# Six of eight chunks of the last up piece, with the upper partitions' half rows moved to the lower ones and loaded from GpSimd's queue

## The chip, the cores and the metric

One NeuronCore of one Trainium2 chip runs the whole program. The metric is the device time of one execution in microseconds; the kernel before has a median of 2686.6 us over three runs. A profiled execution gives the trace from which the lines below come; its own span is 2685.0 us.

## The reference

Two layers, run twice in turn on two tokens (B = 2, one position each, D = 576): attention over a cache of 8192 positions with 32 heads of 128, and a gated mlp with 4608 inner columns. Everything is float32.

```python
def _A_ref(x, k_cache, v_cache, wq, wo):
    q = (x @ wq).reshape(B, Sq, H, Dh).transpose(0, 2, 1, 3)
    scores = einsum("bhqd,bhkd->bhqk", q, k_cache) * (Dh ** -0.5)
    o = einsum("bhqk,bhkd->bhqd", softmax(scores), v_cache)
    return o.transpose(0, 2, 1, 3).reshape(B, Sq, H * Dh) @ wo
def _B_ref(x, w_gate, w_up, w_down):
    g, u = x @ w_gate, x @ w_up
    return (gelu(g) * u) @ w_down
x = x + _A_ref(layernorm(x), k_cache, v_cache, wq, wo)
x = x + _B_ref(layernorm(x), w_gate, w_up, w_down)
x = x + _A_ref(layernorm(x), k_cache, v_cache, wq, wo)
x = x + _B_ref(layernorm(x), w_gate, w_up, w_down)
```

The caches (2 x 268 MB, read in both layers but for some parts that are kept) and the weights make 1153 MB that go from HBM to the core.

## The kernel before

**One large tile.** Keys, values and weights all lie in one SBUF tile, `space`, of 128 partitions by 50,176 columns. The class `Arena` hands out column ranges of it when the program is built. Each load is a function `make` in the list `queue`: `pump` (L148) runs them in order as long as the arena has room, and `done` (L152) frees a range when the last instruction that reads it has been written down, and pumps again. So the order of loads is the order of the list (`plan_first`, `plan_mlp(0)`, `plan_second`, `plan_mlp(1)`), all are issued from SP's queue, and each stands in the program as soon as its place is free. The waits between engines and transfers are put in by the framework, from which columns and partitions of a tile each instruction reads and writes. SP's loads use eight completion semaphores, in turn.

**The second attention's end.** VectorE multiplies keys with the query, GpSimd adds halves (L661), VectorE sums the rest, ScalarE takes the exponential, TensorE multiplies with the values (L762). `project` (L807) then multiplies with the eight pieces of `wo`, and `add_to_x` (L520) adds the result to `x`.

**The second mlp** (`mlp`, L931, with `split` false). `norm` (L486) centres `x`, transposes it into `xt` (128 partitions by 6 + 288 columns; each of nine blocks of 32 columns holds one set of half rows) and lets GpSimd compute `rstd` (L517), which ScalarE first needs in `activate` (L976). The gate and up matrices, 576 by 4608, are read as 1152 half rows of 2304: partition p holds half rows 9p to 9p + 8. `half_rows` (L221) loads them; gate in three transfers of three half rows a partition (3456 KB each), up in two such and three single ones (1152 KB each), as `GU` says. In `all_products` (L959) each half row on the partitions is cut into eight chunks of HG = 288 columns, and one product per chunk, with eight columns of `xt` as weights, adds into the PSUM tile `acc`; `window` picks the columns so that the even and the odd half rows fall on different rows of `acc`. A product in float32 shows as two matmul instructions in the trace. The last piece, the single one with u = 8, is the "ninth half row" of the change: its half rows on even partitions are first halves of a row of up, those on odd partitions second halves.

After it `activate` (L973) runs once for each half of the columns, and the down products (L1004) follow in eight parts, as their weights land (`down`, L264, issued at L271), with idle products (L526) between the first of them. `add_to_x` and two stores end the program.

Of the kernel before, what the change touches and what calls it, by code (L numbers as in the profile page):

```python
# [9 lines left out]
F32 = mybir.dt.float32  # L10
# [31 lines left out]
RING = 5 * SLOT  # L42
END = RING + NPLACE * PLACE
HELD = 5


class Item:
# [75 lines left out]
def decode_layers(ctx, tc, x_in, kc, vc, wq, wo, wg, wu, wd, out):  # L123
# [19 lines left out]


    arena = Arena()
    queue, ready, places = [], {}, {}

    def pump():  # L148
        while queue and queue[0]():
# [2 lines left out]
    def done(key):  # L152
        arena.free(key)
        pump()
# [54 lines left out]
    def weights(key, n, first, transfers):  # L209

        def make():
            at = arena.ring(key, n) if first is None else arena.fit(key, n, first)
            if at is None:
                return False
            t = ready[key] = part_at(at, n)
            transfers(t)
            return True

        queue.append(make)

    def half_rows(key, w, us, first):  # L221

        width = w.shape[1] // 2
        rows = w.rearrange("r (s w) -> (r s) w", w=width).rearrange("(p u) w -> p u w", p=P)

        def transfers(t):
            nc.sync.dma_start(t.rearrange("p (u w) -> p u w", w=width), rows[:, us[0]:us[-1] + 1, :])

        weights(key, len(us) * width, first, transfers)

    def of_half(h, k):

# [166 lines left out]
    def plan_mlp(layer):  # L399
        if layer == 0:  # L400
            for h in range(2):
                for u in range(4):
                    split_rows("g", wg, h, u)
                split_middle(h)
                for u in range(4):
                    split_rows("u", wu, h, u)
        else:
            for g, (name, w) in enumerate((("g", wg), ("u", wu))):
                for us in GU[g]:
                    half_rows((name, layer, us[0]), w, us, 0)  # L410
        for rows in DOWN[layer]:
            down(layer, rows)

# [45 lines left out]

    xt = consts.tile([P, PAD + NU * 32], F32, name="xt")
    nc.vector.memset(xt, 0.0)


# [20 lines left out]
    def norm(split=False, then=None):  # L486
        stats = work.tile([P, 6], F32, name="stats")
        nc.vector.bn_stats(stats, x)
        apart = work.tile([P, 4, 6], F32, name="apart")
        nc.vector.tensor_mul(  # L490
            apart, stats.unsqueeze(1).to_broadcast([P, 4, 6]), strip.unsqueeze(2).to_broadcast([P, 4, 6])
        )
        every4 = small(P, 4 * 6)
        nc.tensor.matmul(every4, same, apart.rearrange("p c t -> p (c t)"), start=True, stop=True)
        mv = work.tile([P, 2], F32, name="mv")
        nc.vector.bn_aggr(mv, every4)
        xc = once.tile([P, CW, 2], F32, name="xc", tag="xc")
        xr = x.rearrange("p (m r) -> p r m", r=NU)
        xs = xc.rearrange("p w s -> p (w s)")
        if split:  # L500
            xm = xs[:, :5 * 32].rearrange("p (u m e) -> p u m e", u=5, e=2)
            parts = [(xm[:, 0:4, :, e], xr[:, 5 * e:5 * e + 4, :], 0) for e in range(2)]
            parts += [(xm[:, 4, :, e], xr[:, 4, :], e) for e in range(2)]
            xs = xs[:, :5 * 32].rearrange("p (u q) -> p u q", u=5)
        else:
            parts = [(xc[:, :, s], x, s) for s in range(2)]
            xs = xs.rearrange("p (q u) -> p u q", u=NU)
        for to, of_x, s in parts:
            nc.vector.tensor_scalar(to, of_x, mv[:, 0:1], side[:, s:s + 1], op0=ALU.subtract, op1=ALU.mult)
        u = xs.shape[1]  # L510
        nc.vector.transpose(xt[:, PAD:PAD + 32 * u].rearrange("p (u q) -> p u q", u=u), xs)
        if then is not None:
            then()
        ve = work.tile([P, 1], F32, name="ve")
        nc.vector.tensor_scalar_add(ve, mv[:, 1:2], EPS)  # L515
        rstd = work.tile([P, 1], F32, name="rstd")
        nc.gpsimd.tensor_tensor(out=rstd, in0=ve, in1=mhalf, op=ALU.pow)  # L517
        return rstd
# [409 lines left out]
        add_to_x()  # L928


    def mlp(layer):  # L931
        split = layer == 0
        rstd = norm(split)
        if split:
            idle_products(3)
        hT = once.tile([P, 2, NI, 2, 2, B], F32, name="hT", tag="xc")

        def window(u, at):

            return xt[:, PAD + 32 * u - at:PAD + 32 * u - at + 4 * B]  # L940

        def split_products(h):

            steps = [(("g", layer, h, u), u, 2, (0,)) for u in range(4)] + [(("gu", layer, h), 4, 1, (0, 1))]
            steps += [(("u", layer, h, u), u, 2, (1,)) for u in range(4)]
            for key, u, sides, gs in steps:
                w = ready.pop(key).rearrange("p (k c w) -> p k c w", c=4, w=HG)
                for k in range(2):
                    g, e = (k, 0) if u == 4 else (gs[0], k)
                    for c in range(4):  # L950
                        nc.tensor.matmul(
                            acc[32 * c:32 * c + 4 * B, h, :HG], window(u, 4 * g + 2 * e), w[:, k, c, :],
                            start=(key == steps[0][0] and k == 0), stop=(key == steps[-1][0] and k == 1),
                        )
                done(key)
                if key != steps[-1][0]:
                    idle_products(1)

        def all_products():  # L959

            for g, name in enumerate("gu"):
                for us in GU[g]:
                    w = ready.pop((name, layer, us[0])).rearrange("p (u v c w) -> p u v c w", v=2, c=4, w=HG)
                    for u in us:
                        for v in range(2):
                            for c in range(4):
                                nc.tensor.matmul(
                                    acc[32 * c:32 * c + 4 * B, v, :HG], window(u, 4 * g), w[:, u - us[0], v, c, :],
                                    start=(g == 0 and u == 0), stop=(g == 1 and u == NU - 1),
                                )  # L970
                    done((name, layer, us[0]))

        def activate(v):  # L973

            o = once.tile([P, 2, HG], F32, name="o", tag="row")
            nc.scalar.activation(o[:, 0, :], acc[:, v, :HG], AF.Copy, scale=rstd)  # L976
            gu = o[:, 1, :].rearrange("p (i r) -> p i r", i=NI)
            nc.vector.transpose(gu, o[:, 0, :].rearrange("p (m i) -> p i m", i=NI))  # L978
            g = gu[:, :, 0:4]
            a = once.tile([P, NI, 4], F32, name="ga", tag="part")  # L980
            nc.vector.tensor_mul(a, g, g)
            nc.vector.tensor_scalar(a, a, 0.044715, 1.0, op0=ALU.mult, op1=ALU.add)
            nc.vector.tensor_mul(a, a, g)
            nc.scalar.activation(a, a, AF.Tanh, scale=math.sqrt(2.0 / math.pi))
            nc.vector.scalar_tensor_tensor(a, a, 1.0, g, op0=ALU.add, op1=ALU.mult)
            nc.vector.tensor_mul(a, a, gu[:, :, 4:8])
            a, to = a.rearrange("p i (e b) -> p (i e) b", b=B), hT[:, v].rearrange("p i e s b -> p (i e) s b")
            nc.vector.tensor_scalar_mul(to[:, :, 0, :], a, 0.5)
            nc.scalar.mul(to[:, :, 1, :], a, 0.5)

        if not split:
            all_products()
        for v in range(2):
            if split:
                split_products(v)
            activate(v)
        for n, rows in enumerate(DOWN[layer]):
            if n < len(IDLE[layer]):
                idle_products(IDLE[layer][n])
            w = ready.pop(("d", layer, rows[0])).rearrange("p (i c) -> p i c", c=D)  # L1000
            for k, (t, i) in enumerate(rows):
                v, e = divmod(t, 2) if split else (t % 2, t // 2)
                for c in range(4):
                    nc.tensor.matmul(  # L1004
                        xps[32 * c:32 * c + 2 * B, :], hT[:, v, i, e, :, :].rearrange("p s b -> p (s b)"),
                        w[:, k, c * CW:(c + 1) * CW],
                        start=(rows is DOWN[layer][0] and k == 0), stop=(t, i) == (NT - 1, NI - 1),
                    )
            done(("d", layer, rows[0]))
        add_to_x()  # L1010
        if layer == 0:
            idle_products(1)
# [34 lines left out]
```

## Time and profile before

| | us |
|---|---|
| median of three runs | 2686.6 (2686.47 to 2687.26) |
| span of the profiled execution | 2685.0 |
| busy: TensorE, VectorE, ScalarE, GpSimd | 914.4, 1806.0, 163.7, 1161.8 |
| moved by DMA | 1154.30 MB, mean 430 GB/s |

The page divides the span into 40 slices and shows each engine's busy share in each. The chain of waits starts at the last instruction and goes back to what released it, and so on; the timeline has one row for each group of like instructions with start, length, engine, line, names and shapes; a row of SPq is an issue, not the transfer. In a table by windows the columns are start and end, length, busy time and count of each engine, the granted TensorE clock, the DMA engines' busy share and GB/s. The lines themselves stand where the prediction uses them.

### The profile page before, as it was taken

The numbers are of one execution on the slowest core, as the hardware profiler recorded it, in microseconds if no ns is written. First come the engines' busy times: TensorE is split into PE (matmuls) and PEld (weight loads), VectorE is DVE, ScalarE is ACT, GpSimd is POOL, SyncE is SP. The second block draws the span as 40 slices with busy tenths as digits, with TensorE's granted clock in tenths as the row PEclk, the third lists the DMA queues.
The fourth block names the chain that finished last, engine by engine and source line by source line (L and its number), as shares of the span: only waits on it lengthen the run. The fifth ranks groups of instructions, "written<-read, shape, count | busy, mean of one in ns | idle before, by whom it ended". The sixth has DMA issues, their size and how long they took to land. (4 is left out here: it accounts for less than half of the span.)

```text
span 2685.0 us, 17174 instructions
## 1 busy us (share of the span) xinstructions
PE 914.4 (34%) x7150; PEld 305.4 (11%) x7150; DVE 1806.0 (67%) x874; ACT 163.7 (6%) x786; POOL 1161.8 (43%) x261
## 2 busy tenths in 40 slices
PE   1323332332233233334663333233223323332356
PEld 0100010010001000111221101001000100010022
DVE  4876687677667766867037877667766776776640
ACT  0000000000000000000026000000000000000000
POOL 2543454354445444544028455445444543454420
PEclk7656666665666566566986665666566656656678
DMA  9999999999999999999999999999999999999998
GB/s 422 436 436 426 437 432 434 433 434 432 433 431 435 436 428 433 436 428 425 414 418 434 431 431 436 431 434 434 437 428 434 434 435 431 431 434 435 433 421 375
DMA packets 33950, 1154.30 MB, mean 430 GB/s; under 512 B 4152, under 2 KB 4176, under 8 KB 5968
## 3 DMA queue, kind: packets, MB, share of 16 engines
q1 hardware_dynamic: 33832, 1153.19, 99.8%
q8 instruction: 56, 0.92, 0.1%
q14 instruction: 22, 0.18, 0.0%
q10 hardware_dynamic: 40, 0.01, 0.0%
HBM read 1153.18 MB, written 0.00 MB: 429 GB/s over the span
## 5 line engine op out<-in xcount | busy, mean ns | idle before, releaser
L661 POOL TENSOR_TENSOR space<-space 128x3072 f32<-128x3072 f32 (+3 forms) x221 | 1128.6, 5107 | 1263.3 <-DVE space L644 1202.5
L644 DVE TENSOR_TENSOR space<-space,bank 128x6144 f32<-128x6144 f32 (+3 forms) x223 | 1112.7, 4991 | 560.2 <-DMA space<-in_A_k_cache_dram 496.8
L762 PE MATMUL acc<-space,prz 128*8 128x512 f32 x4096 | 594.6, 744 | 199.4 <-DMA space<-in_A_v_cache_dram 195.5
L664 DVE TENSOR_REDUCE S<-space 128x48 f32<-128x3072 f32 (+3 forms) x223 | 569.3, 2553 | 89.9 <-POOL space L661 89.6
L592 PE MATMUL bank<-qsb,pick 4*64 4x128 f32 (+1 forms) x256 | 46.3, 436 | 863.1 <-DVE space L644 853.1
L762 PEld LDWEIGHTS acc<-space,prz 128*8 128x8 f32 x4096 | 119.1, 104 | 616.3 <-issue 410.6
L784 PE MATMUL bank<-of,osb 128*32 128x2 f32 x512 | 40.9, 202 | 324.4 <-DVE osb L777 324.4
L713 ACT ACTIVATE nbs<-bank 128x2 f32<-128x2 f32 (+1 forms) x68 | 11.6, 171 | 1848.2 <-PE bank L698 1801.8
L592 PEld LDWEIGHTS bank<-qsb,pick 4*64 4x64 f32 (+1 forms) x256 | 20.7, 202 | 882.5 <-DVE space L644 863.2
L517 POOL TENSOR_TENSOR rstd<-ve,mhalf 128x1 f32<-128x1 f32 x4 | 2.2, 550 | 168.8 <-DVE ve L515 168.8
L690 PE MATMUL bank<-ident,m 128*1 128x128 f32 x68 | 19.5, 286 | 160.7 <-DVE m L688 160.5
L784 PEld LDWEIGHTS bank<-of,osb 128*32 128x32 f32 x512 | 35.9, 154 | 331.7 <-DVE osb L777 330.5
L978 DVE STREAM_TRANSPOSE o<-o 128x288 f32<-128x288 f32 x4 | 2.8, 691 | 94.5 <-ACT o L976 94.5
L729 PE MATMUL bank<-sums,unit 128*128 128x2 f32 x120 | 35.2, 363 | 87.0 <-ACT prz L721 87.0
L776 DVE TENSOR_TENSOR acc<-acc,diag 128x512 f32<-128x512 f32 x64 | 43.5, 680 | 22.0 <-PE acc L762 22.0
L721 ACT ACTIVATE prz<-S,nbs 64x128 f32<-64x128 f32 (+1 forms) x128 | 50.7, 396 | 17.3 <-POOL prz L711 14.4
L803 ACT ACTIVATE oT<-bank,rinv 32x8 f32<-32x8 f32 x110 | 28.5, 259 | 381.5 <-PE bank L784 380.8
L654 ACT ACTIVATE space<-space 128x128 f32<-128x128 f32 x164 | 48.3, 296 | 23.6 <-DVE space L644 21.7
L698 PE MATMUL bank<-m,unit 1*128 1x2 f32 (+1 forms) x136 | 39.0, 354 | 25.3 <-DVE m L696 25.3
L777 DVE TENSOR_REDUCE osb<-acc 128x128 f32<-128x512 f32 x64 | 44.3, 691 | 2.2
L521 DVE TENSOR_TENSOR x<-bank,x 128x144 f32<-128x144 f32 x4 | 1.2, 308 | 64.1 <-PE bank L1004 40.4
L729 PEld LDWEIGHTS bank<-sums,unit 128*128 128x128 f32 x120 | 30.1, 311 | 92.2 <-ACT prz L721 92.2
(73 smaller groups left out, 427.6 us busy)
## 6 DMA issues: line engine op xcount, KB each, us to landing
space<-in_A_v_cache_dram SPq DMA_DIRECT2D x8, 4096.0 KB
space<-in_A_k_cache_dram SPq DMA_DIRECT2D x6, 4096.0 KB
space<-in_A_wo_dram SPq DMA_DIRECT2D x15, 1152.0 KB
space<-in_A_k_cache_dram SPq DMA_DIRECT2D x15, 1024.0 KB
space<-in_B_w_down_dram SPq DMA_DIRECT2D x9, 1152.0 KB
space<-in_B_w_gate_dram SPq DMA_DIRECT2D x3, 3456.0 KB
space<-in_A_v_cache_dram SPq DMA_DIRECT2D x10, 1024.0 KB
space<-in_A_wq_dram SPq DMA_DIRECT2D x3, 3072.0 KB
```

Of the source, the lines that this page charges most:

```text
L592: nc.tensor.matmul(qb[n][to, :], pick[32 * c:32 * c + 4, r:r + 1].to_broadcast([4, P // it.heads]), qsb[32 * c:32 * c + 4, (h % 4) * DH:(h ...
L644: nc.vector.tensor_tensor(out=u[:, :rows, :], in0=t[:, :rows, :], in1=qb[n].unsqueeze(1).to_broadcast([P, rows, DH]), op=ALU.mult)
L654: nc.scalar.activation(u[:, j, :], u[:, j, :], AF.Copy, accum_out=S[n][:, k * JC + j:k * JC + j + 1])
L661: nc.gpsimd.tensor_tensor(out=half, in0=half, in1=u[:, :r, DH // 2:], op=ALU.add)
L664: nc.vector.tensor_reduce(out=S[n][:, k * JC:k * JC + own_rows(n, k, m)], in_=prod.pop((n, k)), axis=AX.X, op=ALU.add)
L698: nc.tensor.matmul(mT[n][:, :heads], ones[0:1, :], m1[:, :heads], start=True, stop=True)
L721: nc.scalar.activation(pr[at, lo:].rearrange("p (g e) -> p g e", e=4)[:, 0:it.rows // 2:2, :], s[at, :it.rows].rearrange("p (g r) -> p g r ...
L729: nc.tensor.matmul(tot[n][:, :ITEMS[n].heads], ones, rs.pop(n), start=True, stop=True)
L762: nc.tensor.matmul(accumulator(n)[32 * c:32 * c + 8, :], pr[:, at:at + 8], t[g // 4][:, g % 4 * 4:g % 4 * 4 + 4, :].rearrange("p j d -> p ...
L776: nc.vector.tensor_tensor(out=q, in0=q, in1=diag.unsqueeze(2).to_broadcast([P, 4, DH]), op=ALU.mult)
L777: nc.vector.tensor_reduce(out=t, in_=q.rearrange("p r d -> p d r"), axis=AX.X, op=ALU.add)
L784: nc.tensor.matmul(po[lo:lo + 32, i, :], t[:, i::GH], of, start=True, stop=True)
```

## The change

Only the last up piece (u = 8) of the second mlp is handled otherwise. `lower_rows` takes the place of `half_rows` for it. Of the 2304 columns of each half row the last two chunks (576 columns) are still loaded from SP's queue, onto all 128 partitions. The first six chunks (1728 columns) are placed on partitions 0 to 63 alone: the half row of partition q and, beside it, that of partition q + 64. These are eight transfers of eight partitions (every fourth one) by two half rows, kept in the list `shift`. `load_shifted`, called at the start of `mlp`, issues them from GpSimd's queue, and behind each of them a transfer of 8 partitions by 2 by 2 numbers of `x_in` into columns of the upper partitions that nothing reads. The piece takes 4040 columns of `space` instead of 2304.

`move_down` copies the four columns of `xt` that belong to u = 8 from the upper to the lower partitions, with a product by the identity and a copy by ScalarE, into four columns added to `xt`. `last_products` does the six chunks as two products over 64 partitions each, and the last two as before.

```diff
+CUT = 6
+    def lower_rows(key, w, u, cut, first):
+        width = w.shape[1] // 2
+        rows = w.rearrange("r (s w) -> (r s) w", w=width).rearrange("(q u) w -> q u w", u=NU)[:, u, :]
+        moved = rows.rearrange("(s a j i) w -> a i j s w", s=2, a=2, i=4)
+        def transfers(t):
+            nc.sync.dma_start(t[:, 2 * (cut + 4):], rows[:, cut:])
+            to = t[:HALF, :2 * (cut + 4)].rearrange("(a j i) (s w) -> a i j s w", a=2, i=4, s=2)
+            apart = t[HALF:HALF + 8, :32 * 8].rearrange("p (n s w) -> n p s w", n=8, s=2)
+            for a in range(2):
+                for i in range(4):
+                    shift.append((to[a, i, :, :, :cut], moved[a, i, :, :, :cut], apart[4 * a + i, :, :, :2]))
+        weights(key, width + cut + 8, first, transfers)
...
-                    half_rows((name, layer, us[0]), w, us, 0)
+                    if name == "u" and us[0] == NU - 1:
+                        lower_rows((name, layer, us[0]), w, us[0], CUT * HG, 0)
+                    else:
+                        half_rows((name, layer, us[0]), w, us, 0)
...
-    xt = consts.tile([P, PAD + NU * 32], F32, name="xt")
+    xt = consts.tile([P, PAD + NU * 32 + 2 * B], F32, name="xt")
...
+    def load_shifted():
+        little = x_in[:, 0, :].rearrange("b (j s w) -> (b j) s w", j=4, s=2)[:, :, :2]
+        for to, rows, beside in shift:
+            nc.gpsimd.dma_start(to, rows)
+            nc.gpsimd.dma_start(beside, little)
+        shift.clear()
     def mlp(layer):
         split = layer == 0
+        load_shifted()
         rstd = norm(split)
...
+        def move_down():
+            first = small(P, 2 * B)[:HALF]
+            at = PAD + 32 * (NU - 1)
+            nc.tensor.matmul(first, ident[HALF:, HALF:], xt[HALF:, at:at + 2 * B], start=True, stop=True)
+            nc.scalar.copy(xt[:HALF, at + 32:at + 32 + 2 * B], first)
+        def last_products():
+            key = ("u", layer, NU - 1)
+            w, side = ready.pop(key), CUT * HG + 4
+            for n in range(8):
+                v, c = divmod(n, 4)
+                to = acc[32 * c:32 * c + 4 * B, v, :HG]
+                if n >= CUT:
+                    at = 2 * side + (n - CUT) * HG
+                    nc.tensor.matmul(to, window(NU - 1, 4), w[:, at:at + HG], start=False, stop=True)
+                    continue
+                for s in range(2):
+                    at = s * side + n * HG
+                    nc.tensor.matmul(
+                        to, window(NU - 1 + s, 4)[:HALF], w[:HALF, at:at + HG], start=False, stop=(s == 1)
+                    )
+            done(key)
         def all_products():
             for g, name in enumerate("gu"):
                 for us in GU[g]:
+                    if name == "u" and us[0] == NU - 1:
+                        last_products()
+                        continue
...
         if not split:
+            move_down()
             all_products()
```

More of the change, by code (lines that the diff above doesn't have):

```diff
@@ L145, in decode_layers @@
     arena = Arena()
-    queue, ready, places = [], {}, {}
+    queue, ready, places, shift = [], {}, {}, []
     def pump():
```

## The prediction

> **What bounds the kernel now.** I read the page first, then the chain of waits, then the last 80 us instruction by instruction.
>
> ```profile
> span 2685.0 us, 17174 instructions
> ...
> DMA  9999999999999999999999999999999999999998
> ...
> q1 hardware_dynamic: 33832, 1153.19, 99.8%
> ```
>
> The DMA engines are busy in all 40 slices, and one queue, SP's, keeps them so. The end of the chain of waits (start, length, what):
>
> ```profile
> 2535.45 46.09 DMA space<-in_A_v_cache_dram
> 2581.61 22.01 DMA space<-in_A_wo_dram
> 2603.68 49.37 DMA space<-in_B_w_up_dram
> 2653.07 27.34 DMA space<-in_B_w_down_dram
> 2680.45 0.67 PE bank L1004 x16
> ...
> 2681.66 0.31 DVE x L521
> ```
>
> From 2535 to 2680 it is transfer after transfer: no engine ends a step. The second mlp in order of time (start, length, engine, line; in brackets the idle time before and what ended it):
>
> ```profile
> 2571.01 2.35 POOL L661 TENSOR_TENSOR space<-space 128x1024 f32<-128x1024 f32 x1 [0.87 <-DVE space L644]
> ...
> 2611.38 0.55 POOL L517 TENSOR_TENSOR rstd<-ve,mhalf 128x1 f32<-128x1 f32 x1 [38.01 <-DVE ve L515]
> ...
> 2614.77 4.56 PE L967 MATMUL acc<-space,xt 128*8 128x288 f32 x48 [5.19 <-DMA space<-in_B_w_gate_dram]
> ...
> 2617.84 38.34 SPq L271 DMA_DIRECT2D space<-in_B_w_down_dram  x8
> ...
> 2622.88 3.10 PE L967 MATMUL acc<-space,xt 128*8 128x288 f32 x48 [3.55 <-DMA space<-in_B_w_gate_dram]
> 2631.08 4.93 PE L967 MATMUL acc<-space,xt 128*8 128x288 f32 x48 [5.10 <-DMA space<-in_B_w_gate_dram]
> ...
> 2639.30 5.93 PE L967 MATMUL acc<-space,xt 128*8 128x288 f32 x48 [3.28 <-DMA space<-in_B_w_up_dram]
> ...
> 2647.54 6.73 PE L967 MATMUL acc<-space,xt 128*8 128x288 f32 x80 [2.31 <-DMA space<-in_B_w_up_dram]
> ...
> 2653.10 0.61 PEld L967 LDWEIGHTS acc<-space,xt 128*8 128x8 f32 x16 [0.36 <-DMA space<-in_B_w_up_dram]
> ...
> 2655.88 1.16 PE L967 MATMUL acc<-space,xt 128*8 128x288 f32 x16 [1.62 <-DMA space<-in_B_w_up_dram]
> ```
>
> Gate and up weights arrive about every 8.2 us by thirds, PE works each off in 3 to 6 us and waits. So 288 matmul instructions (4 x 48 + 80 + 16) are hidden behind loads. Two things carry this cover: PE starts each part as it lands, and SP's eight loads of the down weights are issued from 2617.84 on, long before the up weights are through at 2655.88, so the queue never empties.
>
> **The change part by part.** The last up piece is 1152 KB. Of it 864 KB leave SP's queue and become eight transfers on GpSimd (108 KB each), each followed by a tiny one; 288 KB stay with SP. Bytes are unchanged apart from eight times 128 B. What decides is when GpSimd may issue and who waits for it. The built program of the changed kernel (its own line numbers) reads, with the semaphores each row waits for:
>
> ```
> L955 DMACopy space<-in_B_w_up_dram 8x2x1728 [waits DMAHW3_49,DMAHW4_49,DMAHW2_49,DMAHW5_49,DMAHW1_49,DMAHW6_49,DMAHW0_49,DMAHW7_49,DVE_49,PE_49]   (GpSimd, first)
> L1024 Matmult acc<-space,xt 8x288 [waits DMASW6_49,DMASW4_49,DMAHW2_49,DMASW2_49,DMASW0_49]   (PE, first gate product)
> L288 DMACopy space<-in_B_w_down_dram 128x5184 [waits DMASW4_49,DMASW6_49,DMASW2_49,DMAHW2_49,DMASW0_49,PE_49]   (SP, first down load)
> ```
>
> DMAHW0 to 7 are the eight lanes of SP's loads, DMASW0 to 7 GpSimd's. The destination takes every fourth partition of one large tile (`space`), and the ordering made for it covers everything between its first and last address: all of the other weights. So (a) GpSimd's first transfer waits for the newest load on every SP lane, the last of which is the 288 KB rest of this same piece; (b) PE's first gate product waits for the last four large GpSimd transfers (their lanes at the second count), although its own weights have long landed; (c) so does SP's first down load, and SP issues in order, so the seven behind it wait as well. Nothing hides any of this: the three waits form one serial chain.
>
> Its steps:
>
> 1. Release of GpSimd. The loads up to the seventh up row are untouched; they are issued without waiting for gate products. That row lands at 2653.10, the next 1152 KB took 2655.88 - 2653.10 = 2.78 us, a quarter of it is 0.70: 2653.80.
>
> 2. The GpSimd stretch. No row of before shows a transfer issued by GpSimd. The nearest:
>
> ```profile
> L271 SPq DMA_DIRECT2D space<-in_B_w_down_dram x8: 327/328/328, 2617.8 to 2655.9; - x8
> ```
> ```profile
> SPq L1043 <- DMA out_dram<-x: 1.3, 1, 1.3
> ```
> ```profile
> 2682.00 0.64 SPq L1019 DMA_DIRECT2D out_dram<-x  x1
> ```
>
> An issue on SP takes 0.33; a lone small transfer takes 0.64 + 1.3 = 1.9 from issue to landing. The data of one large transfer take 2.78 x 108/1152 = 0.26 on 16 engines, 0.52 if on eight. Fourteen issues lie ahead of the eighth large one. Lower bound, issues as cheap as SP's: 14 x 0.33 + 0.5 + 1.9 = 7.0. Upper bound, one transfer after the other: 14 x 1.9 + 2.4 = 29. GpSimd's smallest arithmetic above is 0.55; I take 0.8 an issue, the geometric middle of 0.33 and 1.9, nearer to that row than to either end: 14 x 0.8 + 2.4 = 13.6. [...]
>
> 3. All gate and up products, now in one go: 288 - 16 + 28 = 300 instructions (the last piece has twelve half products and two whole ones instead of eight whole). By the rows above 48 take 3.10 warm and 5.93 cold; granted clocks for these stretches:
>
> ```profile
> 2622.00:2627.00 5.00, 3.10 (x48) 1.22 (x48) 1.00 1.02 437
> ...
> 2639.00:2646.00 7.00, 5.93 (x48) 1.69 (x48) 0.56 1.00 424
> ```
> ```profile
> 2647.50:2652.00 4.50, 4.46 (x48) 1.79 (x52) 0.00 (x0) 0.00 (x0) 0.00 (x0) 0.62 1.03 434
> 2652.00:2655.00 3.00, 2.26 (x40) 0.68 (x30) 0.00 (x0) 0.00 (x0) 0.00 (x0) 1.00 1.03 435
> ```
>
> The third column from the right is the granted clock. PE will have idled some 55 us, so it starts cold. A cold start lasts some 4.5 us (the 2647.54 group reaches the full clock at about 2652): 36 instructions at 0.124, then 264 at 0.065: 4.5 + 17.1 = 21.6. Bounds: all warm 19.4, all cold 37.2.
>
> 4. Activation and down products:
>
> ```profile
> 2659.82 0.23 ACT L989 ACTIVATE hT<-ga 128x36 f32<-128x36 f32 x1 [0.49 <-DVE ga L986]
> ...
> 2666.01 1.89 PE L526 MATMUL bank<-prz,ident 128*4 128x256 f32 x8
> ...
> 2668.35 2.39 PE L1004 MATMUL bank<-space,hT 128*4 128x144 f32 x72 [0.45 <-DMA space<-in_B_w_down_dram]
> ...
> 2670.55 1.03 PE L526 MATMUL bank<-prz,ident 128*4 128x256 f32 x4
> 2671.69 1.41 PE L1004 MATMUL bank<-space,hT 128*4 128x144 f32 x40
> ...
> 2672.91 1.03 PE L526 MATMUL bank<-prz,ident 128*4 128x256 f32 x4
> 2674.87 1.16 PE L1004 MATMUL bank<-space,hT 128*4 128x144 f32 x32 [0.93 <-DMA space<-in_B_w_down_dram]
> ...
> 2675.85 0.59 PE L526 MATMUL bank<-prz,ident 128*4 128x256 f32 x2
> 2676.95 0.92 PE L1004 MATMUL bank<-space,hT 128*4 128x144 f32 x24 [0.51 <-DMA space<-in_B_w_down_dram]
> 2679.05 0.92 PE L1004 MATMUL bank<-space,hT 128*4 128x144 f32 x24 [1.18 <-DMA space<-in_B_w_down_dram]
> ...
> 2680.45 1.14 PE L1004 MATMUL bank<-space,hT 128*4 128x144 f32 x24 [0.48 <-DMA space<-in_B_w_down_dram]
> ...
> 2681.16 0.11 PEld L1004 LDWEIGHTS bank<-space,hT 128*4 128x4 f32 x8 [0.36 <-DMA space<-in_B_w_down_dram]
> ```
>
> The last up product ends at 2657.04, the first half of hT at 2660.05: 3.0. The down products with their idle products, back to back at the warm pace: 2 x 2.39 + 1.89 + 1.03 + 1.41 + 1.03 + 1.16 + 0.59 + 0.92 + 0.92 + 1.14 = 14.9. From their end (2681.59) to the end of the span: 3.4.
>
> 5. The down loads run beside 3 and 4. The first goes where the first ten gate products have been read (2.2 us into step 3), starts within 1.9, and 20,736 columns take three times the 8.2 us of a third (2622.88 to 2631.08): 2.2 + 1.9 + 24.6 = 28.7 after the GpSimd stretch. PE's last down product comes at 21.6 + 3.0 + 14.9 = 39.5. The loads are covered by about 10 us; without PE's backlog they would end the run.
>
> Costed at nothing: `move_down` (one product, one ACT copy) lies in PE's 5.19 us wait before 2614.77 and delays nothing, as PE then waits for GpSimd; if it did not, about 0.5 us. `rstd` is now behind GpSimd's sixteen issues, and its reader, ACT, comes only after step 3; were that not so, 0.55. The larger `xt`, its memset: under 0.1 at the start.
>
> Sum: 2653.8 + 13.6 + 21.6 + 3.0 + 14.9 + 3.4 = 2710.3 for the span of this execution; the median of the runs lies 2686.6 - 2685.0 = 1.6 above it: **2711.9**, 25 us or 0.9% slower.
>
> **The rivals.**
>
> *The transfers are free early, and balance the engines.* If the first GpSimd issue came after that engine's last attention work (2573.4) and before SP's first down issue (2617.84, the point that decides), the queue would never empty. What is to be won lies in the tail:
>
> ```profile
> 2674.00:2681.00 7.00, 3.96 (x98) 2.33 (x98) 0.00 (x0) 0.00 (x0) 0.00 (x0) 1.00 0.51 207
> ```
>
> The last two columns are the DMA share and GB/s: half the engines' time is unused there, while others still work. If lower partitions are served by those that end early, 3/4 of the piece's time on the late half, 0.75 x 2.78 = 2.1 us, moves to the early one: 2711.9 becomes 2686.6 - 2.1 = 2684.5, faster by 0.08%. For it: the tail. Against it: wait (a). Chance 0.03. [...]
>
> *The products are not held, only the down loads.* If PE worked gate and up off as they land, the end would be the loads': 2653.8 + 13.6 + 1.9 + 24.6 + 3.8 (from the last landing, 2681.16, to the end) + 1.6 = 2699.3. Against it: wait (b). 0.05.
>
> *Issues are dear,* one transfer after another, step 2 at 29 instead of 13.6: 2727.3. For it: the small transfers' 1.9; against: nothing makes each wait for the one before, only the ninth to sixteenth wait for a lane. 0.08.
>
> *PE stays at half clock* through step 3: 37.2 instead of 21.6: 2727.5. Against: the 2647.54 group turned warm on its own. 0.07.
>
> **How the numbers follow.** Main case 0.77, of its own 2704 (cheap issues, all warm) to 2720. The predicted time is its sum, 2712. The range 2699 to 2725 leaves out the first rival and most of the last two. A difference under 0.2% (5.4 us) can't be told from no change here. Faster 0.01; within 0.2%: 0.03, from the first rival and less; slower 0.96.
>
> **What would show it.** GpSimd's sixteen transfers start near 2654, not near 2574; the DMA share drops to little between there and some 14 us later; the first matmul of the gate weights moves from 2614.77 to about 2667 and some 300 run without waits; the first down issue follows at about 2669; the last rows of the chain of waits are PE's, with no down load ending a wait. Step 2 is wrong if the issues lie closer than 0.4 or wider than 1.5 us. All is wrong if gate products start before 2620.

## The result, and the profile after

| | before | after |
|---|---|---|
| median of the runs, us | 2686.6 | 2708.95 (2708.79 to 2709.53, five runs) |
| ratio, 95% interval | | 1.0083 [1.0071, 1.0095] |
| span of the profiled execution, us | 2685.0 | 2707.1 |

The change costs 22.35 us. All of it lies in the last 110 us of the run. First the page of the changed kernel: its span, the GB/s of the 40 slices and GpSimd's queue (packets, MB, share).

```profile
span 2707.1 us, 17233 instructions
...
GB/s 418 434 434 434 434 434 434 433 433 432 434 432 433 433 433 432 433 427 424 413 419 430 433 433 433 432 433 433 432 434 433 433 432 433 433 432 434 429 428 238
...
q0 software_dynamic: 640, 0.89, 0.1%
```

Thirty-nine slices look as they should; only the last has lost its rate (238, where before had 375). The end of the chain of waits of the changed kernel (start, length, what):

```profile
2606.64 47.24 DMA space<-in_B_w_up_dram
...
2654.80 0.75 POOL space L955
...
2662.20 0.55 POOL space L956
2662.75 2.98 DMA space<-in_B_w_up_dram
2665.72 0.34 issue
2666.06 18.91 PE acc L1024 x272
2684.97 2.05 PE acc L1008 x24
2687.02 0.32 PE acc L1004
...
2690.38 0.24 ACT hT L1046
2690.62 0.04 issue
2690.66 2.39 PE bank L1062 x72
...
2701.33 2.27 PE bank L1062 x64
2703.62 0.31 DVE x L541
```

Before, this stretch of the chain was a transfer of up weights followed by one of down weights, to the end. Now the up transfer releases GpSimd (2653.88), GpSimd issues for 8 us, its last large transfer releases PE, and PE does everything that had been hidden, with no load in the chain any more. Three rows of the timeline of the changed kernel show who waited, and for how long (in brackets):

```profile
2654.80 0.75 POOL L955 DMA_DIRECT2D space<-in_B_w_up_dram  x1 [80.43 <-DMA space<-in_B_w_up_dram]
...
2666.06 6.30 PE L1024 MATMUL acc<-space,xt 128*8 128x288 f32 x64 [53.53 <-DMA space<-in_B_w_up_dram]
...
2669.13 3.13 SPq L288 DMA_DIRECT2D space<-in_B_w_down_dram  x2
```

The first gate product moved from 2614.77 to 2666.06 and the first down issue from 2617.84 to 2669.13, 51.3 us each. The windows of the changed kernel (the last three columns are the granted clock, the DMA share and GB/s) show the queue run dry and fill again:

```profile
2652.00:2654.00 2.00, 0.00 (x0) 0.00 (x0) 0.00 (x0) 0.00 (x0) 0.00 (x0) 0.50 0.17 66
2654.00:2656.00 2.00, 0.00 (x0) 0.00 (x0) 0.00 (x0) 0.00 (x0) 1.21 (x2) 0.50 0.00 0
2656.00:2664.00 8.00, 0.00 (x0) 0.00 (x0) 0.00 (x0) 0.00 (x0) 7.98 (x16) 0.50 0.37 97
...
2668.00:2670.00 2.00, 2.00 (x24) 0.75 (x20) 0.00 (x0) 0.00 (x0) 0.00 (x0) 0.50 0.00 0
2670.00:2675.00 5.00, 5.00 (x84) 2.10 (x79) 0.00 (x0) 0.00 (x0) 0.00 (x0) 0.94 1.01 377
2675.00:2695.00 20.00, 18.19 (x306) 8.52 (x295) 3.71 (x14) 1.82 (x6) 0.00 (x0) 1.00 0.99 419
```

For some 18 us, from 2652 to 2670, the DMA engines do almost nothing but GpSimd's 0.89 MB. The queue thins before that, with 335 GB/s from 2645 to 2650 and 206 from 2650 to 2652.

### The profile page after: what moved, and what is told of

Same layout as the page of the kernel before. It is cut to its first block, busy times and chain, and to the rows that moved or that the text cites. A ratio compares the mean times of both kernels' runs of the same rounds, so it can differ in the third digit from the quotient of the medians.

```text
span 2707.1 us, 17233 instructions
## 1 busy us (share of the span) xinstructions
PE 905.4 (33%) x7164; PEld 304.2 (11%) x7164; DVE 1806.0 (67%) x874; ACT 163.9 (6%) x787; POOL 1170.9 (43%) x277
## 5 line engine op out<-in xcount | busy, mean ns | idle before, releaser
L674 ACT ACTIVATE space<-space 128x128 f32<-128x128 f32 x164 | 48.3, 296 | 23.6 <-DVE space L664 21.6
L955 POOL DMA_DIRECT2D space<-in_B_w_up_dram x8 | 4.6, 581 | 80.4 <-DMA space<-in_B_w_up_dram 80.4
```

The lines of the kernel that those rows point to most:

```text
L674: nc.scalar.activation(u[:, j, :], u[:, j, :], AF.Copy, accum_out=S[n][:, k * JC + j:k * JC + j + 1])
```

## The experiments

Two questions were open. Which part of the serial chain costs what? And would the placement have paid if no false wait had come with it? The first four runs take the chain apart. Of the other eight, six take the waits away, and two cut the same load in the kernel before, where no such wait exists.

### The chain taken apart

**One small transfer that GpSimd must wait with.** The kernel before, with the ninth rows of up loaded as ever, and one transfer of 128 B from GpSimd into every fourth partition of 32 columns beside them.

```diff
+            shift.append(t[0:32:4, width:width + 32].rearrange("p (s w) -> p s w", s=2)[:, :, :2])
...
+        for to in shift:
+            nc.gpsimd.dma_start(to, little)
```

> The kernel before with one tiny transfer from GpSimd (every fourth of 32 partitions) into unread columns at the start of the second mlp; in the built program it waits for all eight lanes of SP's loads, and nothing but GpSimd's own next instruction (rstd) waits for it. Theory: GpSimd's wait alone costs nothing, since rstd, some 2 us after 2655.9, is needed by ScalarE only at 2657.2 and the activation has 2 us before the first down weights land: 2686.6 to 2687.2. Rival (the late GpSimd work itself is the loss): 2690 or more.

Measured: 2686.53, ratio 0.9999 [0.999, 1.0008]. GpSimd's row in its timeline:

```profile
2656.54 0.75 POOL L949 DMA_DIRECT2D space<-in_A_x_dram  x1 [83.77 <-DMA space<-in_B_w_down_dram]
```

GpSimd waits 83.8 us, much as in the changed kernel (80.4), and `rstd` behind it is late as well, and neither costs anything. GpSimd's own wait is not the loss; what waits for GpSimd is.

**The down loads held, the products not.** The same, with the columns beside the ninth rows widened, so that the first down load falls into what GpSimd's transfer covers (the edit is against the run above).

```diff
-            shift.append(t[0:32:4, width:width + 32].rearrange("p (s w) -> p s w", s=2)[:, :, :2])
-        weights(key, width + 32, first, transfers)
+            shift.append(t[0:32:4, width:width + 3464].rearrange("p (s w) -> p s w", s=2)[:, :, :2])
+        weights(key, width + 3464, first, transfers)
```

> The kernel before with one tiny transfer from GpSimd into unread columns, its two runs 1732 columns apart; in the built program it waits for all SP lanes, and SP's first down load waits for it, but no product does. Theory (the down loads alone held): last up landing 2655.9, 3.3 for the tiny transfer, 28.2 from the first down issue to the last landing, 3.8 to the end, 1.6 from span to median: 2692.8, so some 6 of the 22 us without a product held. Rival (a late down queue costs nothing because half of the engines idled at the end anyway): 2686.6.

Measured: 2693.37, ratio 1.0025 [1.0015, 1.0035]. Its timeline:

```profile
2656.31 1.16 PE L990 MATMUL acc<-space,xt 128*8 128x288 f32 x16 [1.55 <-DMA space<-in_B_w_up_dram]
...
2659.01 4.08 SPq L282 DMA_DIRECT2D space<-in_B_w_down_dram  x8
...
2668.28 4.50 PE L1027 MATMUL bank<-space,hT 128*4 128x144 f32 x72 [9.11 <-DMA space<-in_B_w_down_dram]
```

The products of gate and up are done at 2657, as before; the down loads start at 2659 on an empty queue, and PE waits 9.1 us for the first of them. So holding the down loads behind a single small transfer is worth 6.7 of the 22.3 us. The remaining 15.6 are what is left for the fifteen further issues and the products that wait with them; no run takes this remainder apart wholly; the next one measures seven of the issues.

**The changed kernel without the tiny transfers.**

```diff
             nc.gpsimd.dma_start(to, rows)
-            nc.gpsimd.dma_start(beside, little)
```

> The changed kernel without the eight tiny transfers; all waits stay. Theory (the stretch on GpSimd is bound by its issues, 0.556 us each, fourteen of them before the eighth large one): seven issues fewer, 3.9 us, 2709.0 becomes 2705.1. Rival (bound by the data on eight engines, or by the wait for a lane): under 1 us less, 2708 or more.

Measured: 2705.32, ratio 1.0069 [1.0054, 1.0084], that is 3.6 less than with them. From its chain of waits:

```profile
2654.77 4.05 POOL space L955 x7
2658.82 3.04 DMA space<-in_B_w_up_dram
2661.86 0.24 issue
2662.11 7.90 PE acc L1023 x85
```

Seven issues fewer lie ahead of the last large transfer, at 0.556 us each 3.9 us, and PE starts at 2662.11 instead of 2666.06, 3.95 earlier. The issues are the price of GpSimd's stretch, one for one.

**The changed kernel without the idle products between the down products.**

```diff
-    IDLE = [(2, 2, 2, 2, 2, 2, 2, 2, 1), (4, 4, 2, 2, 1)]
+    IDLE = [(2, 2, 2, 2, 2, 2, 2, 2, 1), (4, 0, 0, 0, 0)]
```

> The changed kernel without the nine idle products between the parts of the down products. Theory (PE's backlog ends the run, the last down load lands at 2697.8 and PE ends at 2703.5): their 3.3 us on the chain of waits go, 2709.0 becomes 2705.7. Rival (the down loads end the run): no difference.

Measured: 2705.84, ratio 1.0072 [1.0055, 1.0089], 3.1 less than the changed kernel. The end of its chain:

```profile
2692.79 4.94 PE bank L1062 x153
2697.73 0.52 issue
2698.25 2.17 PE bank L1062 x63
2700.45 0.31 DVE x L541
```

Taking work from PE shortens the run by what it took, and the down products then run nearly without a gap. So PE's backlog ends the changed kernel, not the loads.

### The waits taken away

**Eight neighbouring partitions instead of every fourth.** Each large transfer now covers a closed block of partitions, so the ordering made for it touches nothing else: in the built program neither the first gate product nor the first down load waits for a transfer of GpSimd's any more.

```diff
-        moved = rows.rearrange("(s a j i) w -> a i j s w", s=2, a=2, i=4)
+        moved = rows.rearrange("(s a i j) w -> a i j s w", s=2, a=2, i=4)
...
-            to = t[:HALF, :2 * (cut + 4)].rearrange("(a j i) (s w) -> a i j s w", a=2, i=4, s=2)
+            to = t[:HALF, :2 * (cut + 4)].rearrange("(a i j) (s w) -> a i j s w", a=2, i=4, s=2)
```

> Everything of the change is kept (six chunks on the lower partitions, sixteen transfers from GpSimd, half products), but each large transfer fills eight neighbouring partitions instead of every fourth one; in the built program the first gate product and the first down load then wait for no GpSimd transfer, and GpSimd's first one waits only for the former readers of its own columns. Theory (the loss is the chain of three waits): GpSimd issues from about 2605 us on, products and down loads run as before, 2684.5 us if the engines serving the lower partitions end early, at most 2688.7 if they end late. Rival (GpSimd's issues, the placement or the half products cost by themselves): above 2700.

Measured: 2699.79, ratio 1.0048 [1.0036, 1.0061], which is what neither side had expected. The waits are gone, and 13.2 us of loss remain. GpSimd's first issue in its timeline, and three windows of it:

```profile
2602.21 0.74 POOL L955 DMA_DIRECT2D space<-in_B_w_up_dram  x1 [29.01 <-PE bank L832]
```
```profile
2605.00:2625.00 20.00, 8.26 (x84) 3.40 (x84) 2.42 (x8) 0.16 (x1) 4.08 (x8) 0.57 1.01 346
2625.00:2645.00 20.00, 8.80 (x76) 2.73 (x80) 0.00 (x0) 0.00 (x0) 2.79 (x5) 0.61 1.02 361
2645.00:2665.00 20.00, 9.22 (x92) 2.83 (x88) 0.00 (x0) 0.00 (x0) 0.00 (x0) 0.67 0.99 383
```

GpSimd's transfers now start at 2602 and run beside SP's loads. The DMA engines stay busy (share 1.0), but they move 346 to 383 GB/s where the run otherwise has some 430. Over 60 us that is 4.0 MB less, 9 us at 430 GB/s. Busy is not the same as fast.

**The same without the tiny transfers, and with each tiny one ahead of its large one.**

```diff
             nc.gpsimd.dma_start(to, rows)
-            nc.gpsimd.dma_start(beside, little)
```
```diff
-            nc.gpsimd.dma_start(to, rows)
             nc.gpsimd.dma_start(beside, little)
+            nc.gpsimd.dma_start(to, rows)
```

> As e1_contiguous without the tiny transfers. If a transfer of eight rows goes to eight DMA engines in turn and the tiny ones only step past the other eight, then the large ones now alternate between both halves and shift no load: 2686.6, about 2 us above e1. If the tiny ones do nothing for the engines: the same as e1 within 0.5.

> As e1_contiguous with each tiny transfer ahead of its large one. If eight engines in turn is right, the large ones now load the other half of the engines: 2688.7, some 2 us above before and 4 above e1, if e1 gained; the reverse if e1 lost. If turns do not matter: the same as e1.

Measured: 2698.77, ratio 1.0044 [1.0031, 1.0056], and 2702.45, ratio 1.0058 [1.0045, 1.0071]. The tiny transfers and their order shift the end by 1 to 4 us. Their order does matter (2.7 us between tiny behind and tiny ahead), but the run without them doesn't lie between the two, and none of the values expected came out, so what they do to single DMA engines stays open. The 12 us remain without any of them.

**Which of three: the queue, the number of partitions, or the layout as such.** Three runs were put side by side. One GpSimd transfer of all 64 lower partitions; the eight transfers of eight neighbouring partitions from ScalarE; and the 64 partitions in one transfer from SP, so that there is no second queue at all. The edits, shortened: the first and the second against the run of eight neighbouring partitions, the third against the first.

```diff
-        moved = rows.rearrange("(s a i j) w -> a i j s w", s=2, a=2, i=4)
+        moved = rows.rearrange("(s p) w -> p s w", s=2)
...
-            for a in range(2):
-                for i in range(4):
-                    shift.append((to[a, i, :, :, :cut], moved[a, i, :, :, :cut], apart[4 * a + i, :, :, :2]))
+            to = t[:HALF, :2 * (cut + 4)].rearrange("p (s w) -> p s w", s=2)
+            shift.append((to[:, :, :cut], moved[:, :, :cut]))
...
-            nc.gpsimd.dma_start(beside, little)
```
```diff
-            nc.gpsimd.dma_start(to, rows)
-            nc.gpsimd.dma_start(beside, little)
+            nc.scalar.dma_start(to, rows)
```
```diff
-            shift.append((to[:, :, :cut], moved[:, :, :cut]))
+            nc.sync.dma_start(to[:, :, :cut], moved[:, :, :cut])
```

> GpSimd loads the lower partitions' rows in one transfer of 64 partitions (0.88 MB) in place of eight transfers of eight neighbouring partitions, without the tiny ones; nothing waits for it falsely, as with the contiguous layout. Theory A (the new loss of the contiguous layout, 12 to 13 us, comes from all engines writing into eight neighbouring partitions at once): the rows of the transfer now go all over the lower partitions, so 2685.5 to 2689.5, and the moved bytes stay near 430 GB/s from 2600 to 2660. Theory B (it comes from a second queue of software descriptors beside SP's, whatever partitions it writes): 2694 to 2700, and the rate falls to 320 to 380 GB/s again while the DMA share stays at 1.0.

> The eight transfers of eight neighbouring partitions of the contiguous layout, issued by ScalarE in place of GpSimd, without the tiny ones (against 2698.8 with GpSimd). Theory A (eight neighbouring partitions): the loss stays, 2696 to 2701. Theory B (GpSimd's software descriptors): the loss goes, 2685.5 to 2689.5. If any second queue beside SP's costs it: this one stays near 2698 and the single GpSimd transfer does too.

> The same layout and the same products on half the partitions (48 matmul instructions more or less as in the changed kernel, and the rows moved down through PE and ScalarE), the lower rows loaded by SP in one transfer of 64 partitions right behind the rest of the item. All theories: no second queue, so 2685.5 to 2688.5, that is what layout and products cost by themselves (up to 2 us). If the layout itself were the cost, it would lie at 2694 or more here too.

Measured:

| rows on the lower partitions, loaded by | us | ratio | above before, us |
|---|---|---|---|
| GpSimd, one transfer of 64 partitions | 2692.43 | 1.0021 [1.0012, 1.003] | 5.6 |
| SP, one transfer of 64 partitions | 2693.33 | 1.0025 [1.0015, 1.0035] | 6.5 |
| GpSimd, eight transfers of eight neighbours, no tiny ones | 2698.77 | 1.0044 [1.0031, 1.0056] | 12.2 |
| ScalarE, eight transfers of eight neighbours, no tiny ones | 2698.97 | 1.0047 [1.0034, 1.006] | 12.1 |

The queue makes no difference: GpSimd and ScalarE, GpSimd and SP agree within a microsecond. What differs between 6 and 12 us is the form: one transfer of 64 partitions, or eight of eight. So partitions per transfer and number of transfers change together, and no run separates them. GpSimd's single transfer lies in neither theory's range, and that 64 partitions from SP's own queue would cost 6.5 us too was expected by none. A window of the kernel before, and then those of the run with SP's single transfer, show the place:

```profile
2650.00:2660.00 10.00, 7.13 (x80) 2.48 (x72) 1.84 (x7) 0.91 (x4) 0.00 (x0) 0.90 1.02 436
```
```profile
2640.00:2645.00 5.00, 5.00 (x48) 1.58 (x40) 0.00 (x0) 0.00 (x0) 0.00 (x0) 0.50 0.99 418
2645.00:2650.00 5.00, 2.59 (x32) 0.87 (x28) 0.00 (x0) 0.00 (x0) 0.00 (x0) 0.84 1.01 303
2650.00:2655.00 5.00, 3.82 (x44) 1.16 (x36) 0.00 (x0) 0.00 (x0) 0.00 (x0) 0.81 1.03 257
2655.00:2660.00 5.00, 1.17 (x16) 0.34 (x16) 0.00 (x0) 0.00 (x0) 0.00 (x0) 0.88 1.06 219
2660.00:2665.00 5.00, 1.27 (x12) 0.49 (x16) 0.00 (x0) 0.00 (x0) 0.00 (x0) 0.50 0.97 303
2665.00:2670.00 5.00, 5.00 (x26) 1.30 (x19) 0.56 (x1) 0.50 (x1) 0.00 (x0) 0.50 0.98 418
```

For 20 us the rate falls, to about half (219) at the lowest, at a DMA share of 1.0 throughout.

**The same bytes without a move.** Two last runs leave data, products and places as in the kernel before and only cut the load of the ninth rows: once by columns, over all 128 partitions, once also between partitions 63 and 64.

```diff
+            if key[0] == "u" and key[1] == 1 and key[2] == NU - 1:
+                cut = 6 * HG
+                nc.sync.dma_start(t[:, cut:], rows[:, us[0], cut:])
+                nc.sync.dma_start(t[:, :cut], rows[:, us[0], :cut])
+                return
```
```diff
-                nc.sync.dma_start(t[:, :cut], rows[:, us[0], :cut])
+                for at in (0, HALF):
+                    nc.sync.dma_start(t[at:at + HALF, :cut], rows[at:at + HALF, us[0], :cut])
```

> The kernel before with the load of the ninth rows of the second up cut at the same column into two SP transfers, both over all 128 partitions: the same bytes and 128 pieces of 6912 B as in the transfer of 64 partitions that cost 6.5 us, each piece where it lay before. Theory P (the loss belongs to the partitions written): 2686 to 2688. Theory D (it belongs to one more transfer of pieces of 6912 B, or to the issue): 2691 to 2694.

> The same, but the 0.88 MB go in two SP transfers of 64 partitions, the lower rows to the lower partitions and then the upper rows to the upper ones: in the sum no partition gets more than before. If the loss comes from the sum alone (64 partitions take 0.88 MB, of which half is new to them): 2686 to 2688. If it comes from each transfer that all engines write into only 64 partitions while it lasts (0.88 MB in all here, as in the transfer that cost 6.5 us): 2690 to 2694.

Measured: 2686.95, ratio 1.0 [0.9991, 1.0009], and 2693.89, ratio 1.0026 [1.0016, 1.0035]. The same stretch of both, first over all partitions, then in two halves:

```profile
2650.00:2655.00 5.00, 5.00 (x56) 1.76 (x52) 0.00 (x0) 0.00 (x0) 0.00 (x0) 0.64 1.04 435
2655.00:2660.00 5.00, 3.57 (x36) 1.13 (x28) 1.51 (x6) 0.73 (x2) 0.00 (x0) 1.00 1.00 427
```
```profile
2650.00:2655.00 5.00, 3.31 (x48) 1.02 (x40) 0.00 (x0) 0.00 (x0) 0.00 (x0) 0.95 1.04 278
2655.00:2660.00 5.00, 1.26 (x16) 0.34 (x16) 0.00 (x0) 0.00 (x0) 0.00 (x0) 0.74 1.04 233
```

Pieces of 6912 B and one more issue cost nothing. Two transfers of 64 partitions cost 7.0 us, although each partition gets exactly what it got before. So the loss is not in the sum of bytes per partition; it belongs to each transfer that covers only half of the partitions, while it lasts. GpSimd's single one shows how long that is: 20.2 us from its issue at 2603.08 to its landing, and the rate of that run is 345, 267, 282 and 365 GB/s in the four windows of 5 us from 2605 to 2625, and 435 in the next. And since the old layout and products lose as much here as the new ones did with SP's single transfer (6.5), the new layout and the half products add nothing that these runs can tell. No version with the rows moved beat the kernel before.

## Why the prediction was right, point by point

The forecast was 2711.9, the median is 2708.95. Its steps, against the chain of the changed kernel:

| step of the prediction | predicted, us | measured, us |
|---|---|---|
| 1, release of GpSimd, at | 2653.8 | 2653.88 |
| 2, the GpSimd stretch | 13.6 | 11.84 |
| gap between 2 and 3 | 0 | 0.34 |
| 3, all gate and up products | 21.6 | 21.57 |
| 4, activation | 3.0 | 3.03 |
| 4, down products | 14.9 | 12.94 |
| tail to the end of the span | 3.4 | 3.5 |
| span | 2710.3 | 2707.1 |
| median above span | 1.6 | 1.85 |

Step 1 held: the transfer of up weights in the chain ends at 2653.88. The false waits (a), (b) and (c) that were read from the built program all show in the trace, and they are the mechanism: with closed blocks of partitions GpSimd starts at 2602 and PE and SP no longer wait for it. That returns 9.2 of the 22.3 us (2708.95 to 2699.79) and not all of them, because the transfers then meet SP's loads. Of (c) the trace shows one thing more. The first down issue came at 2669.13, 3.4 after the last landing on GpSimd's queue (2665.72), because it also waits for the first gate products, which (b) held (SP's longest wait for them shows as 3.3 us); step 5 had counted 2.2 us for these products, and 3.1 passed.

Step 2 was too long by 1.8. An issue on GpSimd takes 0.556 us and not the guessed 0.8; fourteen of them, the first longer at 0.75, make 8.0 instead of 11.2. What the sum lacked is the 0.92 us from the release to the first issue (2653.88 to 2654.80), and the last large transfer took 2.98 from its issue to the landing, against 2.4. So an error of 3.2 was offset by half, which is luck.

Step 3 held to a tenth, with the cold start as forecast: in the windows the clock is 0.50 until 2670 and 0.94 over the next five microseconds. That it held so closely is luck in part. The first 272 instructions took 18.91, where the prediction's paces give 4.5 + 236 x 0.065 = 19.8. The 24 of the half products, priced like whole ones at 1.6, took 2.05, and the last four, with an idle product between them, 0.6 instead of 0.3.

Step 4 held for the activation. The down products took 2.0 less, since I had added up the busy times of groups that overlap at their ends when they run back to back. In the timeline of the changed kernel the first group is busy to 2693.05, and the next starts at 2692.87:

```profile
2690.66 2.39 PE L1062 MATMUL bank<-space,hT 128*4 128x144 f32 x72 [1.81 <-ACT hT L1046]
2692.87 1.67 PE L546 MATMUL bank<-prz,ident 128*4 128x256 f32 x7
```

This term and step 2 make 3.7 us, of which the gap and the smaller terms take back 0.5: the miss of 3.2 in the span.

Step 5 held in kind: no down load ends a wait in the chain. In size it was too generous. The last down weights come in at 2697 to 2698, so PE's end at 2703.6 covers them by about 6 us, not 10:

```profile
2696.00:2697.00 1.00, 1.00 (x28) 0.68 (x20) 0.00 (x0) 0.00 (x0) 0.00 (x0) 1.00 0.16 62
2697.00:2698.00 1.00, 1.00 (x22) 0.56 (x24) 0.00 (x0) 0.00 (x0) 0.00 (x0) 1.00 0.02 9
2698.00:2699.00 1.00, 1.00 (x31) 0.76 (x25) 0.00 (x0) 0.00 (x0) 0.00 (x0) 1.00 0.00 0
```

The terms costed at nothing hold as far as the runs can show it: `rstd` came late in the run where GpSimd alone waited, and that was free.

Of the rivals, the one that ends on the other side had the larger error. "Free early" was priced at a gain of 2.1 us, from the idle half of the engines in the tail; that the lower partitions are served by engines of their own was the author's assumption, and no run shows it. When the transfers really were early, they lost 5.6 us (one transfer) to 15.9 us (eight, each behind its tiny one): the share of the engines' time was a poor measure of what a transfer into few partitions would cost them. Whether the moved rows went through a part of the engines alone stays open: during SP's transfer of 64 partitions the mean share of all sixteen was 0.97 to 1.06, but the loads around it may have kept the other engines busy. "Only the down loads held" is a different case from the run that held them, where just one small transfer stood ahead; there the loads did end the run, as that rival's mechanism says. "Issues one after another" falls by the 0.556 us, "half clock" by the 0.94 above.

Open: the placement on every fourth partition has not been run without the false waits, with a tile of its own for these rows; so the loss of that very layout when it runs beside SP's loads is not known. Nor is it known why a transfer into 64 partitions costs about three times its own extra time (below).

## What to carry to other kernels

A transfer whose destination skips partitions of a large shared tile can be ordered as if it wrote everything between its ends (closed blocks in place of every fourth partition took 2708.95 to 2699.79 us here): read in the built program who waits for it before pricing its bytes. Moving bytes between partitions to balance DMA engines did not pay here, beside a full queue, when the transfers that carried them covered half of the partitions or fewer (5.6 to 15.9 us lost); cutting the same load by columns, on all 128, cost nothing (2686.95 against 2686.89). And look at GB/s beside the DMA share, since a share of 1.0 hid a rate that had halved here (219 GB/s at 1.06, against 436 at 1.02 before).

## What the runs showed of the hardware

**Transfers into few partitions slow the loads beside them.** Three forms of the same 0.88 MB beside SP's full queue: 128 partitions cost nothing (2686.95), 64 cost 5.6 to 7.0 us, eight at a time 12.1 to 15.9. The lowest rate of five microseconds is 219 GB/s with 64 partitions, half of 430; it counts all that moved in its window, the loads over 128 partitions too. If only the 0.88 MB moved at half rate, that would be 2.1 us more (an estimate from 0.88 MB and 430 GB/s); the windows show a low rate for 20 us. The single DMA packets of the traces show that the loads beside were slow too. SP's gate and up loads of three half rows, which cover all 128 partitions, go in packets of 27,648 B. After 2600 us one of them took 1.03 us on the mean before, 1.14 beside GpSimd's one transfer of 64 partitions, and 1.30 and 1.26 beside the eight narrow ones (without tiny ones) of GpSimd and ScalarE. Summed and divided by sixteen engines that is 4.3, 10.7 and 9.2 us more, out of losses of 5.6, 12.2 and 12.1. The page of GpSimd's one transfer agrees: its own 144 packets took 0.1% of the span of 2690.8 us on sixteen engines, at most 4.0 us with the rounding, of which 2.1 are what 0.88 MB take at 430 GB/s; so some 3.7 of the 5.6 us at the least lie with the loads beside it. No run shows what it is in a transfer into few partitions that slows the others.

**An issue on GpSimd.** 0.557 us each, back to back, for a transfer of 108 KB and for one of 128 B alike (557/557/572 ns for the tiny ones), and 0.33 us on SP. The group of the large ones in the changed kernel (min, median, max in ns):

```profile
L955 POOL DMA_DIRECT2D space<-in_B_w_up_dram x8: 557/557/747, 2654.8 to 2662.8; - x8
...
DMA to landing us min/median/max: 2.7/2.9/3.0
```

With SP's queue run dry such a transfer lands 2.9 us after its issue. With issues 1.1 us apart for each large one, the DMA engines got 97 GB/s out of it (the window from 2656 to 2664): the issuing engine set the rate. With seven issues fewer ahead of it the last large transfer landed at 2661.86 instead of 2665.72.
